# Attention with two gated MLPs behind it: a pair's value products in one run of eight, one turn later

## The chip, the cores and the metric

The kernel runs on one core of one Trainium2 chip. The metric is the device time of one execution in microseconds (us); the median of three runs of the kernel before is 1239.47 us (1239.21 to 1240.27). Five engines work beside each other, each through its own list of instructions in order: TensorE (PE, matrix products and transposes; PEld is its weight load), VectorE (DVE), ScalarE (ACT), GpSimd (POOL) and SyncE (SP, whose queue issues most of the DMAs). They meet at semaphores.

## The reference

```python
def _attn_ref(q, k, v, g_q, g_k):          # 4 batches, 12 heads, 448 positions, 64 wide
    q_n, k_n = (rmsnorm(q, g_q), rmsnorm(k, g_k))
    scores = scale * np.matmul(q_n, k_n.transpose(0, 1, 3, 2))
    scores = scores - np.max(scores, axis=-1, keepdims=True)
    attn = np.exp(scores)
    attn = attn / (np.sum(attn, axis=-1, keepdims=True) + 1e-09)
    return np.matmul(attn, v).astype(np.float32)
...
    x = np.ascontiguousarray(attn_out.transpose(0, 2, 1, 3)).reshape(B * S, H * D)
    x = _moe_ref(x=x, **moe_kwargs)        # (x @ w_a) * (x @ w_b) @ w_out
    return _moe2_ref(x=x, **moe2_kwargs)   # sigmoid(x @ w_gate) * (x @ w_val) @ w_out
```

The change lies in the attention. The two MLPs behind it take the rest of the time.

## The kernel before

The attention works on 24 pairs of heads (two heads of one batch, 64 columns each, side by side in 128 partitions). The 448 positions of a head are three chunks of 128 and a rest of 64; the rests of both heads share a chunk. For a pair, the scores are made in seven pieces of 128 x 448 (`s`, four products on PE), each with its row maximum (`top`, DVE) and its exponential (`exp`, ACT, which also adds up the rows). The exponentials must be transposed before they can be multiplied with v: `x_tr(i, j, z)` transposes chunk j in two parts z on PE, into a tile of PSUM, and `x_out` copies that to `pt` in SBUF (ACT for z = 0, DVE for z = 1). `pv(i, part)` multiplies: part 0 takes the chunks j = 0 and 1 of both heads, part 1 takes j = 2 and the shared rest j = 3. Each of these products is two PE instructions with 64 columns of weights, so a part is eight instructions and a pair sixteen. They add up in one PSUM tile `pv`. `norm` (DVE) multiplies it with the reciprocal sums `rs`, which come by way of `rsum` (DVE), `rsum_tr` (a transpose on PE), `rsum_post` (a copy on ACT at L390 and a DMA to DRAM) and `rsum_get` (DMAs that spread the row over the partitions); `put` stores the result.

The Tile framework is told to keep the order in which the functions are called (a manual schedule), so the tuples `begin`, `first`, `turns` and `end` set the order of work by hand: an entry (f, o, ...) calls f for pair i + o. `first` is turn i = 1, `turns` the turns 2 to 22, `end` the rest, in which the first MLP begins. In a turn the scores and exponentials of pair i are made, the exponentials of pair i - 1 transposed, and q and k of pair i + 2 normalised (`mean`, `rsqrt`, `newton`, `scale`) and transposed (`t_tr`), with `k_hi`, `k_lo`, `q_hi`, `q_lo` as their evictions from PSUM on ACT and DVE. From turn 6 on `decode` puts two steps of the first MLP's weight preparation into a turn (L639 on ACT; L640, L642, L646 on DVE). In the turns 15 to 20 `early_hi` (L428, ACT) and `early_lo` (L434, POOL) split finished columns of the attention for the first MLP.

Buffers that matter: all transposes (`x_tr`, `t_tr`, `rsum_tr`, ten tiles in a turn) share three PSUM tiles (`ps_tr`); the scores have four (`ps_s`), `pv` one; `pt` has four buffers for the chunks 0 to 2 and two for the rest; `v` has three.

Lines in the profile: x_tr is L339 and L342 for j < 3 (a turn's first transpose is the L339 of x_tr(-1, 0, 0)) and L344 to L347 for j = 3; x_out is L356 on DVE and L358 on ACT; s L311, top L317, exp L329, pv L371, rsum_tr L385, t_tr L264 to L269, k_hi L284, q_hi L274, norm L406, mean L213 and L214, rsqrt L221 and L222.

Of the kernel before, what the change touches and what calls it, by code (L numbers as in the profile page):

```python
# [23 lines left out]
def attention_then_two_gated_mlps(  # L24
# [90 lines left out]
    def attention():  # L115
# [336 lines left out]
        def mlp(i, n):  # L452
# [20 lines left out]
            (scale, 2, 0), (scale, 2, 2), (top, 0, 5), (rsum, -1), (exp, 0, 5), (x_tr, -1, 1, 0), (x_out, -1, 1, 0),  # L473
            (x_tr, -1, 1, 1), (x_out, -1, 1, 1), (s, 0, 2), (s, 0, 3), (squares, 3),
            (x_tr, -1, 2, 0), (top, 0, 2), (x_out, -1, 2, 0), (exp, 0, 2), (x_tr, -1, 2, 1), (rsum_tr, -1), (top, 0, 6), (exp, 0, 6),
            (x_out, -1, 2, 1), (rsum_post, -1), (pv, -1, 0), (top, 0, 3), (t_tr, 2, 1), (exp, 0, 3), (mean, 3), (rsqrt, 3), (x_tr, -1, 3, 0),
            (k_hi, 2), (newton, 3), (k_lo, 2), (t_tr, 2, 0), (x_out, -1, 3, 0), (q_hi, 2), (q_lo, 2), (k_ends, 2),
        )

        turns = (  # L480
            (rsum_get, -2), (early, 0), (put, -3), (s, 0, 0), (s, 0, 1),
            (x_tr, -1, 0, 0), (x_tr, -1, 0, 1), (top, 0, 0), (x_out, -1, 0, 0), (exp, 0, 0), (top, 0, 4),
            (exp, 0, 4), (x_out, -1, 0, 1), (pv, -2, 1), (scale, 2, 1), (scale, 2, 0), (scale, 2, 2), (top, 0, 1),
            (exp, 0, 1), (load, 4), (load_r, 3), (load_v, 1), (x_tr, -1, 1, 0), (top, 0, 5), (rsum, -1), (exp, 0, 5),
            (x_out, -1, 1, 0), (x_tr, -1, 1, 1), (norm, -2), (x_out, -1, 1, 1), (s, 0, 2),
            (s, 0, 3), (decode, 0, 0), (early_hi, -1), (squares, 3), (early_lo, -1), (x_tr, -1, 2, 0),
            (top, 0, 2), (x_out, -1, 2, 0), (exp, 0, 2), (x_tr, -1, 2, 1), (rsum_tr, -1), (top, 0, 6), (exp, 0, 6), (x_out, -1, 2, 1), (rsum_post, -1),
            (pv, -1, 0), (top, 0, 3), (t_tr, 2, 1), (exp, 0, 3), (decode, 0, 1), (mean, 3), (rsqrt, 3), (x_tr, -1, 3, 0),
            (k_hi, 2), (newton, 3), (k_lo, 2), (t_tr, 2, 0), (x_out, -1, 3, 0), (q_hi, 2), (q_lo, 2), (k_ends, 2),
        )  # L490

        end = (
            (rsum_get, -3), (put, -4), (s, -1, 0), (s, -1, 1), (x_tr, -2, 0, 0), (x_tr, -2, 0, 1), (top, -1, 0),
            (exp, -1, 0), (rsum, -2), (x_out, -2, 0, 0), (top, -1, 4), (exp, -1, 4), (x_out, -2, 0, 1), (pv, -3, 1),
            (top, -1, 1), (exp, -1, 1), (x_tr, -2, 1, 0), (top, -1, 5), (x_out, -2, 1, 0), (x_tr, -2, 1, 1),
            (exp, -1, 5), (x_out, -2, 1, 1), (rsum_tr, -2), (norm, -3), (s, -1, 2), (rsum_post, -2), (s, -1, 3),
            (x_tr, -2, 2, 0), (top, -1, 2), (x_out, -2, 2, 0), (exp, -1, 2), (x_tr, -2, 2, 1), (top, -1, 6),
# [767 lines left out]
    with tc.manual_schedule():  # L1265
        main = mlps()
        attention()
        open_places(6, 4, 2, 3)
        begin_mm("mm1", 3)
        for c in range(KC):  # L1270
            stage_in(0, "A22", c)
        ready[0] = True
        for _ in main:
            pass
# [29 lines left out]
```

## Time and profile before

| | |
|---|---|
| median of three runs | 1239.47 us (1239.21 to 1240.27) |
| the profiled execution | 1240.79 us, span 1239.0 us |
| granted TensorE clock, mean over the span | 0.990 |
| busy in the span: PE, DVE, ACT, POOL | 1199.2, 923.9, 653.5, 158.0 us |
| turns 2 to 22 of the attention | from 39.42 to 267.34 us |

The profiled execution is one run with the hardware profiler; its span reaches from the first to the last instruction, and 1.8 us lie around it. Times in the rows are microseconds from the start of the span. A group of rows in order of time shows a start, a duration, the engine, the line, the operation, the tiles it writes and reads, the shapes and how many like instructions follow each other (x6); in brackets stands the idle time of the engine ahead of it and what ended it.

### The profile page before, as it was taken

Reading aid. Unit: us, or ns where it says so; the run is one execution under the profiler, and the core shown is the slowest. Engines: PE = TensorE matmul, PEld = TensorE weight load, DVE = VectorE, ACT = ScalarE, POOL = GpSimd, SP = SyncE. Lnnn points to the kernel's source line nnn. Section 1 sums busy time; section 2 is a strip of 40 time slices with the busy share of each in tenths; the row PEclk is TensorE's granted clock in tenths of the full one; section 3 lists DMA queues with packets and bytes.
Section 4 is the critical chain, followed back from the end, with each engine's and each line's share of the span. In section 5 each row is a group of like instructions: output and inputs, shape, how many; then the busy total and the mean of one; then the engine's idle time right before and its main releaser. Section 6 shows DMA issues by size and latency. Waiting matters only on the chain.

```text
span 1239.0 us, 18146 instructions
## 1 busy us (share of the span) xinstructions
PE 1199.2 (97%) x6414; PEld 1013.5 (82%) x6414; DVE 923.9 (75%) x1621; ACT 653.5 (53%) x1271; POOL 158.0 (13%) x240
## 2 busy tenths in 40 slices
PE   4999999999899999999999999999999999999997
PEld 3666666667688888888888888788888888999997
DVE  6788889964976786876668789966876877666572
ACT  4778787873643444334445565544445344444542
POOL 4656667700000000000000000000000000000000
PEclk9999999999899999999999999999999999999999
DMA  5244455327134664653865664224654654867583
GB/s 131 74 133 127 136 152 155 119 68 266 48 100 136 189 194 142 195 174 124 305 219 188 196 216 131 94 88 135 195 190 142 207 162 137 280 215 250 170 270 101
DMA packets 142026, 203.00 MB, mean 164 GB/s; under 512 B 23240, under 2 KB 116592, under 8 KB 141936
## 3 DMA queue, kind: packets, MB, share of 16 engines
q1 hardware_dynamic: 140496, 201.26, 51.5%
q8 instruction: 50, 0.82, 0.3%
q10 hardware_dynamic: 1440, 0.59, 0.2%
q14 instruction: 40, 0.33, 0.1%
HBM read 147.46 MB, written 54.35 MB: 163 GB/s over the span
## 4 chain that ended last, share of the span: by engine, by line
PE 67%; DVE 3%; ACT 2%; DMA 1%; issue 1%; SPq 0%; ACTq 0%; DVEq 0%
PE mm L899 44%; PE mm L1176 12%; PE mm L1186 10%; DVE xl L576 1%; DMA u<-gd 0%; DMA wd<-d 0%; SPq L1242 0%; DVE u L812 0%; ACT xh L803 0%; DVE al L812 0%; DVE wl L576 0%; ACTq L1242 0%; ACT mm L1157 0%; ACT ah L1213 0%; ACT gh L1092 0%
## 5 line engine op out<-in xcount | busy, mean ns | idle before, releaser
L899 PE MATMUL mm<-xh,wh 128*128 128x512 f32 (+1 forms) x1008 | 370.2, 367 | 5.6 <-ACT u L955 2.0
L899 PE MATMUL mm<-xl,wh 128*128 128x512 f32 (+1 forms) x1008 | 370.7, 368 | 4.2 <-DVE xl L576 4.2
L899 PE MATMUL mm<-xh,wl 128*128 128x512 f32 (+1 forms) x1008 | 371.8, 369 | 1.1 <-DVE wl L576 1.1
L899 PEld LDWEIGHTS mm<-xh,wh 128*128 128x128 f32 x1008 | 190.8, 189 | 31.2 <-ACT u L955 2.3
L899 PEld LDWEIGHTS mm<-xl,wh 128*128 128x128 f32 x1008 | 190.7, 189 | 28.6 <-DVE xl L576 5.9
L899 PEld LDWEIGHTS mm<-xh,wl 128*128 128x128 f32 x1008 | 190.5, 189 | 23.4 <-DVE wl L576 2.3
L576 DVE TENSOR_TENSOR wl<-d,wh 128x384 fp32r<-128x384 f32 x252 | 137.7, 553 | 74.0 <-ACT wh L1055 45.1
L744 ACT CAST wh<-d 128x384 fp32r<-128x384 f32 x168 | 83.0, 513 | 107.3 <-DVE d L732 75.1
L646 DVE SCALAR_TENSOR_TENSOR d<-d,raw 128x384 uint32<-128x384 uint32 x140 | 82.0, 586 | 52.0 <-ACT d L639 46.1
L639 ACT ACTIVATE d<-raw 128x384 f32<-128x384 f32 x140 | 76.8, 554 | 75.3 <-DMA raw<-in_moe_w_out_dram 42.0
L329 ACT ACTIVATE P<-s,nm 128x448 f32<-128x448 f32 x168 | 105.3, 636 | 9.0 <-DVE nm L317 8.5
L1055 ACT CAST wh<-d 128x384 fp32r<-128x384 f32 x84 | 43.2, 514 | 119.6 <-issue 39.2
L1186 PE MATMUL mm<-wh,gh 128*128 128x384 f32 x294 | 99.4, 338 | 2.5 <-ACT al L1201 2.2
L317 DVE TENSOR_REDUCE nm<-s 128x1 f32<-128x448 f32 x168 | 97.5, 615 | 3.5 <-PE s L311 3.5
L1186 PE MATMUL mm<-wl,gh 128*128 128x384 f32 x294 | 99.3, 338 | 0.0
L1186 PE MATMUL mm<-wh,gl 128*128 128x384 f32 x294 | 99.2, 337 | 0.0
L1176 PE MATMUL mm<-gl,wh 128*128 128x512 f32 x252 | 92.6, 368 | 0.0
L1176 PE MATMUL mm<-gh,wl 128*128 128x512 f32 x252 | 92.4, 366 | 0.0
L1176 PE MATMUL mm<-gh,wh 128*128 128x512 f32 x252 | 91.7, 364 | 0.0
L642 DVE SCALAR_TENSOR_TENSOR raw<-raw 128x384 uint32<-128x384 uint32 x140 | 78.2, 559 | 4.0
L358 ACT COPY pt<-tr 128x512 f32<-128x512 f32 x96 | 55.0, 573 | 44.8 <-PE tr L342 40.9
L969 DVE TENSOR_TENSOR u<-mm,u 128x896 f32<-128x896 f32 x48 | 52.2, 1088 | 30.5 <-PE mm L899 30.4
(149 smaller groups left out, 1938.4 us busy)
## 6 DMA issues: line engine op xcount, KB each, us to landing
gd<-u SPq DMA_DIRECT2D x60, 448.0 KB
u<-gd SPq DMA_DIRECT2D x60, 448.0 KB
d<-wd SPq DMA_DIRECT2D x132, 192.0 KB
raw<-in_moe_w_out_dram SPq DMA_DIRECT2D x48, 384.0 KB
wd<-d SPq DMA_DIRECT2D x72, 192.0 KB
raw<-in_moe_w_a_dram SPq DMA_DIRECT2D x24, 384.0 KB
raw<-in_moe_w_b_dram SPq DMA_DIRECT2D x24, 384.0 KB
raw<-in_moe_w_val_dram SPq DMA_DIRECT2D x23, 384.0 KB
```

Source lines behind the costliest of these rows:

```text
L317: nc.vector.tensor_reduce(out=d["nm"][:, t:t + 1], in_=d["ps"][t], axis=AX.X, op=ALU.max, negate=True)
L329: nc.scalar.activation(out=e, in_=d["ps"].pop(t), func=AF.Exp, bias=d["nm"][:, t:t + 1], accum_out=d["sum"][:, t:t + 1])
L358: nc.scalar.copy(out=d["pt"][j][:, w], in_=tr)
L576: eng.tensor_tensor(out=lo, in0=t, in1=f32(hi), op=ALU.subtract)
L639: nc.scalar.activation(out=f32(t), in_=f32(high), func=AF.Copy, scale=2.0 ** -112)
L642: nc.vector.scalar_tensor_tensor(out=low, in0=high, scalar=0x80000000, in1=low, op0=ALU.bitwise_and, op1=ALU.bitwise_or)
L646: nc.vector.scalar_tensor_tensor(out=t, in0=t, scalar=3, in1=low, op0=ALU.logical_shift_left, op1=ALU.bitwise_or)
L744: nc.scalar.copy(out=hi, in_=t)
L899: nc.tensor.matmul(ps[:, o:o + size], w[:, P * c:P * c + P], x[:, o:o + size], start=(p in (1, 5) and c == 0 and z == 0), stop=(c == KC - ...
L969: nc.vector.tensor_tensor(out=u, in0=ps, in1=u, op=ALU.add)
L1176: nc.tensor.matmul(ps[:, o:o + size], w[:, P * un:P * un + P], g[:, o:o + size], start=(p in (1, 5) and f == 0 and z == 0), stop=(f == HF ...
L1186: nc.tensor.matmul(ps[:, o:o + HB], g[:, P * t:P * t + P], w, start=(p in (1, 5) and f == 0 and z == 0), stop=(f == HF - 1 and z == 2), sk ...
```

## The change

In `first` and `turns` the entry `(pv, -1, 0)`, which stood behind `rsum_post`, is gone. In `turns` `(pv, -2, 0)` stands in front of `(pv, -2, 1)` in the next turn, behind `x_out(-1, 0, 1)`; in `end` `(pv, -3, 0)` in front of `(pv, -3, 1)`. So in the turns both parts of a pair, eight products in sixteen instructions, follow each other. The last two pairs are multiplied in `end` as before.

```diff
@@ first
-            (x_out, -1, 2, 1), (rsum_post, -1), (pv, -1, 0), (top, 0, 3), (t_tr, 2, 1), (exp, 0, 3), (mean, 3), (rsqrt, 3), (x_tr, -1, 3, 0),
+            (x_out, -1, 2, 1), (rsum_post, -1), (top, 0, 3), (t_tr, 2, 1), (exp, 0, 3), (mean, 3), (rsqrt, 3), (x_tr, -1, 3, 0),
@@ turns
-            (exp, 0, 4), (x_out, -1, 0, 1), (pv, -2, 1), (scale, 2, 1), (scale, 2, 0), (scale, 2, 2), (top, 0, 1),
+            (exp, 0, 4), (x_out, -1, 0, 1), (pv, -2, 0), (pv, -2, 1), (scale, 2, 1), (scale, 2, 0), (scale, 2, 2), (top, 0, 1),
...
-            (pv, -1, 0), (top, 0, 3), (t_tr, 2, 1), (exp, 0, 3), (decode, 0, 1), (mean, 3), (rsqrt, 3), (x_tr, -1, 3, 0),
+            (top, 0, 3), (t_tr, 2, 1), (exp, 0, 3), (decode, 0, 1), (mean, 3), (rsqrt, 3), (x_tr, -1, 3, 0),
@@ end
-            (exp, -1, 0), (rsum, -2), (x_out, -2, 0, 0), (top, -1, 4), (exp, -1, 4), (x_out, -2, 0, 1), (pv, -3, 1),
+            (exp, -1, 0), (rsum, -2), (x_out, -2, 0, 0), (top, -1, 4), (exp, -1, 4), (x_out, -2, 0, 1), (pv, -3, 0), (pv, -3, 1),
```

## Rows read from the trace of the kernel before

**Rows 1.** Busy by stretch: turns 2-14, 15-21, 17, 22 (columns in the first row).

```profile
core 0: us, PE busy (x) PEld busy (x) DVE busy (x) ACT busy (x) POOL busy (x), PEclk, DMA share, GB/s
39.42:178.69 139.27, 139.27 (x951) 89.40 (x949) 119.64 (x277) 107.99 (x309) 84.86 (x132) 1.00 0.45 127
178.69:257.57 78.88, 75.50 (x513) 48.15 (x511) 70.65 (x145) 62.33 (x167) 54.64 (x73) 1.00 0.44 134
201.10:212.93 11.83, 10.82 (x74) 6.88 (x74) 10.88 (x23) 8.96 (x25) 8.71 (x11) 1.00 0.53 153
257.57:267.34 9.77, 9.77 (x67) 5.94 (x65) 6.87 (x15) 6.65 (x19) 0.00 (x0) 1.00 0.22 68
```

**Rows 2.** PE in order of time, turn 10 (start, us, engine, line).

```profile
125.13 0.33 PE L339 MATMUL tr<-ident,P 128*128 128x128 f32 x1
...
127.86 0.82 PE L342 MATMUL tr<-ident,P 128*128 128x128 f32 x6
...
130.12 0.27 PE L339 MATMUL tr<-ident,P 128*128 128x128 f32 x1
...
130.88 0.27 PE L385 MATMUL tr<-ident,rc 128*7 128x128 f32 x1
131.09 1.72 PE L371 MATMUL pv<-pt,v 128*64 128x448 f32 x8
132.74 0.55 PE L264 MATMUL tr<-ident,qkn 128*128 128x128 f32 x3
...
133.89 0.49 PE L264 MATMUL tr<-ident,qkn 128*128 128x128 f32 x3
...
135.84 0.33 PE L339 MATMUL tr<-ident,P 128*128 128x128 f32 x1
```

**Rows 3.** ACT in order of time, second half of turn 10.

```profile
130.76 0.59 ACT L358 COPY pt<-tr 128x512 f32<-128x512 f32 x1 [0.99 <-PE tr L342]
...
132.47 0.24 ACT L390 COPY row<-tr 7x128 f32<-7x128 f32 x1
132.62 0.62 ACT L329 ACTIVATE P<-s,nm 128x448 f32<-128x448 f32 x1
...
134.56 0.52 ACT L358 COPY pt<-tr 128x448 f32<-128x448 f32 x1
```

**Rows 4.** All engines in order of time, second half of turn 11.

```profile
141.80 0.56 DVE L356 COPY pt<-tr 128x384 f32<-128x384 f32 x1
...
142.80 0.55 DVE L646 SCALAR_TENSOR_TENSOR d<-d,raw 128x384 uint32<-128x384 uint32 x1
...
145.07 0.52 ACT L358 COPY pt<-tr 128x448 f32<-128x448 f32 x1
```

**Rows 5.** ACT in order of time, second half of turn 2.

```profile
45.05 0.59 ACT L358 COPY pt<-tr 128x512 f32<-128x512 f32 x1 [0.95 <-PE tr L342]
...
48.43 0.52 ACT L358 COPY pt<-tr 128x448 f32<-128x448 f32 x1
```

**Rows 6.** All engines in order of time, turn 17's end and turn 18's first transpose.

```profile
208.67 1.96 DVE L646 SCALAR_TENSOR_TENSOR d<-d,raw 128x384 uint32<-128x384 uint32 x1
...
212.35 0.52 ACT L358 COPY pt<-tr 128x448 f32<-128x448 f32 x1
...
212.93 0.33 PE L339 MATMUL tr<-ident,P 128*128 128x128 f32 x1 [1.01 <-ACT pt L358]
```

**Rows 7.** Weight loads (PEld) of turn 10's run of products, behind its first four.

```profile
131.52 0.14 PEld L371 LDWEIGHTS pv<-pt,v 128*64 128x64 f32 x2 [0.23 <-issue]
131.89 0.14 PEld L371 LDWEIGHTS pv<-pt,v 128*64 128x64 f32 x2 [0.23 <-issue]
```

**Rows 8.** DVE in order of time, turn 10, norm (L406) and x_out(2,1) (L356).

```profile
128.61 0.62 DVE L406 TENSOR_TENSOR xs<-pv,rs 128x448 f32<-128x448 f32 x1 [0.33 <-DMA rs<-dr]
...
131.15 0.54 DVE L356 COPY pt<-tr 128x384 f32<-128x384 f32 x1
```

**Rows 9.** ACT in order of time, end of turn 1.

```profile
38.46 0.52 ACT L358 COPY pt<-tr 128x448 f32<-128x448 f32 x1
```

## The prediction, made before the changed kernel was run

> **What bounds the kernel now.** The page gives TensorE (PE) by far the largest share of busy time. A share is an average over stages, so I read next the busy time of each engine in stretches of the attention [rows 1]. I call the stretch between the first transposes of two turns of the loop a turn. From 39.42 to 178.69, turns 2 to 14, PE has no idle time at all: 139.27 us busy of 139.27, 10.71 us a turn, VectorE (DVE) 119.64, ScalarE (ACT) 107.99. From 178.69 to 257.57, turns 15 to 21, PE is idle for 3.4 of 78.88 us. So for thirteen turns PE's own list is the bound; then something else joins in. Third, I read PE in order of time through turn 10 [rows 2] and ask of each step whom it waits for and who waits for it. Fourth, I follow ACT and DVE from the eviction x_out(2,0) to the eviction x_out(3,0) [rows 3 to 5]: there each step waits for the one before it. Last, the turns in which PE does wait show what closes the circle: a turn's first transposes started 0.06 us after the last turn's x_out(3,0) had ended (212.35 + 0.52 to 212.93), with 1.01 us of idle PE put down to it [rows 6]. Transposes write to three tiles in PSUM, and here the new turn takes the one that x_out(3,0) empties.
>
> The reader should see two things. In turn 10 the chain from x_out(2,0) at 130.76 ends with x_out(3,0) at 134.56 + 0.52 = 135.08, and PE comes to the next turn only at 135.84: 0.76 us of slack [rows 2, 3]. And PE spends the middle of that chain, 131.09 to 132.74, on the four value products (eight PE instructions) of pv(-1, 0). This filler is what the change takes out.
>
> **What the change does to PE's work.** No instruction is added or removed, no DMA is touched; each pair's eight instructions of part 0 go from behind rsum_tr to a place ahead of part 1 in the next turn.
> - Taken out: from rsum_tr at 130.88 to t_tr(2, 1) at 132.74 PE takes 1.86 us [rows 2]. Without the run the next transpose follows at the pitch of transposes, 0.11 (six of them took 0.82 from 127.86, the last alone 0.27: 0.55 / 5). That saves 1.75, and about 0.05 more because the first transpose after products is slow (125.13 is 0.33 long, 130.12 and others 0.27).
> - Put in: a run of eight takes 1.65 (131.09 to 132.74), of which the first pair step takes 0.43 (131.09 to 131.52) and an inner one 0.37 [rows 2, 7]. Eight more inside a run are four inner steps, 4 x 0.375 = 1.50.
> - Balance: 1.80 - 1.50 = 0.30 us less PE work a turn, 10.41 for 10.71: one entry and one exit of a run saved.
>
> The Trainium skill, "TensorEngine Tiling (Array Packing)", section Key Properties, has a rule that fits this: changing the tiling mode drains the array, and the products use 64-column tiles where the transposes use 128. The trace agrees (0.20 us from rsum_tr to the first product, 0.11 between transposes). If PE's work alone counted, that rule would make the kernel faster by the second rival's amount.
>
> **What it does to the order.** All that PE does between x_tr(1,0) and rsum_tr comes 1.50 us later in its turn. Counted from the turn's first transpose, x_tr(2,0) goes from 130.12 - 125.13 = 5.00 to 6.50 [rows 2]. ACT's x_out(2,0) follows it by 0.64 (130.12 to 130.76), so it goes to 7.14; ACT waits there for PE already now, 0.99 us [rows 3], so nothing on ACT takes the delay up. DVE's x_out(2,1) goes from 141.80 - 135.84 = 5.96 to 7.46 [rows 2, 4]. Ahead of it on DVE stand the norm, which reads the products, then x_out(1,1), a weight step and two maxima, and all of them wait for PE in turn. With the norm's own 0.62 they take 131.15 - 128.61 = 2.54 us, so about 2.0 from x_out(1,1) on [rows 8]; x_tr(1,1) ends at 128.68 - 125.13 = 3.55 now [rows 2] and at 5.06 then, so they are through at 7.1, covered by 7.46; without that cover each tenth over would go into the turn. The issue of v's load on the SP queue waits for the products, as now, 1.5 us later; behind it stand loads that are wanted a turn or more later: nothing.
>
> From there the chain is as long as it is now, and three circles close on the next first transpose:
> - Turns in which ACT decodes weights (line 639, between the exponentials and the rsqrt): 134.56 + 0.52 - 130.76 = 4.32 [rows 3]. 7.14 + 4.32 + 0.05 = **11.51**.
> - Turns in which DVE does (L646): from x_out(2,1) at 141.80 to 145.07 + 0.52 = 3.79 [rows 4]. 7.46 + 3.79 + 0.05 = **11.30**.
> - Turns without weights: 48.43 + 0.52 - 45.05 = 3.90 [rows 5], so 11.09. There PE itself is later: t_tr(2, 0) takes the PSUM tile that the copy of the sums (L390) frees, and that copy ends 132.47 + 0.24 - 130.76 = 1.95 after x_out(2,0) starts [rows 3], at 9.09; from t_tr(2, 0) to the next turn PE needs 135.84 - 133.89 = 1.95 [rows 2], and one slow first step of 0.05. 9.09 + 0.05 + 2.00 = **11.14**.
> All three exceed 10.71 although PE has less to do: with the filler gone from where the evictions run, PE has transposes alone for three buffers, and waits.
>
> **The sum**, made against the profiled run:
> - Turn 1 loses a run and gains none. Its x_out(3,0) ends at 38.46 + 0.52 = 38.98 behind a chain that the run isn't part of, so turn 2 starts at 39.04 for 39.42: -0.4 [rows 1, 9].
> - Turns 2 to 5 have no weights: 4 x (11.14 - 10.71) = +1.7.
> - Turns 6, 8, 10, 12, 14 have L639: 5 x 0.80 = +4.0. Turns 7, 9, 11, 13 have L646: 4 x 0.59 = +2.4.
> - Turns 15 to 21 last 78.88 [rows 1]. In 15 to 20 ACT and GpSimd (POOL) also prepare the next stage. In turn 17 L646 took 1.96 us, beside POOL's L434, for 0.55 in turn 11 [rows 4, 6], and the turn lasted 11.83 [rows 1]. L434 doesn't move within such a turn, so L646 starts later and ends at the same point: 11.83 in 15, 17 and 19, 11.51 in 16 and 18, 11.14 in 20 and 21. Together 80.8: +1.9.
> - Turn 22 has no t_tr and lasts 9.77, all of it PE [rows 1]. Its second half of s needs the PSUM tile of exp(0, 3), which ends 132.62 + 0.62 - 130.76 = 2.48 after x_out(2,0) starts [rows 3], and takes 0.71 itself (half of the 1.42 that is left of those 1.95 behind the four transposes): 7.14 + 2.48 + 0.05 + 0.71 = 10.38: +0.6.
> - The end, where PE has no gap either, has one run longer by 1.50: +1.5.
> Sum: -0.4 + 1.7 + 4.0 + 2.4 + 1.9 + 0.6 + 1.5 = **+11.7 us**. The MLPs behind are unchanged and PE's, so all of it reaches the end. The profiled run took 1240.79, 1.3 above the median of the runs: 1252.5 for a profiled run, **1251.2** for the median.
>
> **The rivals.**
> 1. Milder. If the new turn's first transposes take another PSUM tile than x_out(3,0)'s, the copy of the sums alone binds: 11.14 in turns 2 to 14, 13 x 0.43 = 5.6; 15 to 21 at least 1.5, turn 1 and the end as above: +8.8, 1248.3. For it: the order in which tiles come free isn't written in the kernel. Against: the waits of this kind name x_out(3,0) [rows 6].
> 2. Faster: the cover holds. If the chain behind x_out(2,0) fits into the new turn, PE stays the bound and 0.30 is saved in the 17 turns outside 15 to 19: -5.1, 1234.4. It decides where the chain takes under 10.41 - 7.14 - 0.05 = 3.2 us; the rows say 3.8 to 4.3, and on ACT its steps run end to end.
> 3. Heavier: the norm waits for the sums that a DMA spreads (rs). In turn 10 it did, 0.33 us. The sums leave ACT 1.50 us later in a turn. The cover left on DVE is 7.46 - 7.06 = 0.4; a landing 0.9 us beyond what the norm can bear costs 0.5 in each of the nine turns with weights: +4.3, 1255.5. For it: that one wait. Against: it is the only one of its size.
> That the products don't become one run can be left out: the operands of all eight are from the turn before.
>
> The Trainium skill, "Perfetto Trace Analysis", section Optimization Strategy, says that one gap repeating on the engine that should be saturated can mean too few buffers. Turns 2 to 14 show no such gap now; by my sum each gets 0.7 to 1.1 us of them.
>
> **Chances.** Forecast 0.68, milder 0.14, heavier 0.08, the cover holds 0.06, loss and saving cancel 0.04. About 0.2% (2.5 us) is what a measurement can tell from no change: faster 0.06, same 0.04, slower 0.90. The range runs from 1243.5 (milder, with the turns without weights hardly delayed and 15 to 22 as before) to 1257.0 (heavier); some 0.17 lies outside.
>
> **What would show it.** In the changed trace: 16 value products end to end in about 3.16 us; turns of 11.1 to 11.5 us from 39 us on; idle PE ahead of the first transposes put down to x_out(3,0), and ahead of t_tr; x_out(2,0) 7.1 us into a turn; turn 17 still near 11.8. Turns of 10.4 without gaps would show the second rival, turns over 11.6 with DVE waiting for rs the third. I am wrong if PE waits in fewer places, or if the start of the MLPs takes some of the delay back.

## The result, and the profile after

The changed kernel takes **1254.18 us** (median of four runs, 1252.39 to 1255.54) against 1239.87 (1239.21 to 1241.31) for the kernel before beside it: 1.0108 times as long, interval [1.0095, 1.0121]. That is +14.3 us where +11.7 was forecast (1251.2, range 1243.5 to 1257.0). The profiled execution took 1254.91 us.

The first reading is that of [rows 1]: busy time by stretch. The rows are turns 2 to 5 (no weights), 6 to 14 (weights), 15 to 21 (weights and the next stage), then turn 17 alone and turn 22.

```profile
core 0: us, PE busy (x) PEld busy (x) DVE busy (x) ACT busy (x) POOL busy (x), PEclk, DMA share, GB/s
39.29:83.89 44.60, 43.28 (x292) 27.80 (x292) 35.35 (x81) 32.80 (x93) 25.39 (x40) 1.00 0.35 99
83.89:187.57 103.68, 98.06 (x659) 62.58 (x658) 85.89 (x197) 78.17 (x217) 59.34 (x90) 1.00 0.45 128
187.57:268.50 80.93, 76.08 (x511) 48.70 (x512) 65.95 (x144) 63.60 (x168) 54.99 (x74) 1.00 0.44 130
210.95:222.81 11.86, 10.90 (x73) 6.96 (x74) 10.19 (x23) 9.13 (x25) 8.75 (x11) 1.00 0.52 154
268.50:279.14 10.64, 10.12 (x66) 6.08 (x65) 8.14 (x18) 7.26 (x21) 0.10 (x1) 1.00 0.21 64
```

TensorE had no idle time in turns 2 to 14 before; now it is idle for 1.32 us of turns 2 to 5 and for 5.62 us of turns 6 to 14. It is no longer the bound there, and neither is another engine: DVE is busy for 85.89 of 103.68. What is left is a chain across engines.

PE in order of time through turn 10, the turn of [rows 2]:

```profile
130.15 0.33 PE L339 MATMUL tr<-ident,P 128*128 128x128 f32 x1
...
131.06 2.48 PE L371 MATMUL pv<-pt,v 128*64 128x448 f32 x12
133.37 0.92 PE L371 MATMUL pv<-pt,rz 128*64 128x448 f32 x4
134.22 0.33 PE L339 MATMUL tr<-ident,P 128*128 128x128 f32 x1
...
136.67 0.27 PE L339 MATMUL tr<-ident,P 128*128 128x128 f32 x1
...
137.43 0.27 PE L385 MATMUL tr<-ident,rc 128*7 128x128 f32 x1
138.03 0.52 PE L264 MATMUL tr<-ident,qkn 128*128 128x128 f32 x3 [0.33 <-ACT pt L358]
138.90 0.33 PE L344 MATMUL tr<-swap,P 128*128 128x128 f32 x1
139.50 0.49 PE L264 MATMUL tr<-ident,qkn 128*128 128x128 f32 x3
...
141.93 0.33 PE L339 MATMUL tr<-ident,P 128*128 128x128 f32 x1 [0.42 <-ACT pt L358]
```

The sixteen products run end to end from 131.06 to 134.22, 3.16 us as worked out. Where eight of them stood before, between rsum_tr (L385) and t_tr(2, 1) (L264), PE now waits 0.33 us for x_out(2, 0), and at the end of the turn 0.42 for x_out(3, 0) (L358 both). ACT through the second half of that turn, the rows of [rows 3]:

```profile
137.30 0.59 ACT L358 COPY pt<-tr 128x512 f32<-128x512 f32 x1 [1.39 <-PE tr L342]
...
139.12 0.24 ACT L390 COPY row<-tr 7x128 f32<-7x128 f32 x1
139.41 0.64 ACT L329 ACTIVATE P<-s,nm 128x448 f32<-128x448 f32 x1
140.03 0.53 ACT L639 ACTIVATE d<-raw 128x384 f32<-128x384 f32 x1
...
141.36 0.52 ACT L358 COPY pt<-tr 128x448 f32<-128x448 f32 x1
```

x_out(2, 0) starts 137.30 - 130.15 = 7.15 us into the turn (7.14 forecast), x_out(3, 0) ends at 141.88, and the next turn's first transpose starts 0.05 later. The lengths of all turns, each from first transpose to first transpose:

| | before | forecast | after |
|---|---|---|---|
| turns 2 to 5 | 10.71 | 11.14 | 11.15, 11.16, 11.13, 11.16 |
| turns 6, 8, 10, 12, 14 (L639) | 10.71 | 11.51 | 12.13, 11.50, 11.78, 11.51, 11.50 |
| turns 7, 9, 11, 13 (L646) | 10.71 | 11.30 | 11.31 or 11.32 each |
| turns 15, 17, 19 | 11.12, 11.83, 11.85 | 11.83 | 11.88, 11.86, 11.88 |
| turns 16, 18 | 11.29, 11.30 | 11.51 | 11.50, 11.50 |
| turns 20, 21 | 10.75, 10.74 | 11.14 | 11.17, 11.14 |
| turn 22 | 9.77 | 10.38 | 10.64 |

The first product of the MLPs comes at 293.31 for 280.00: 13.3 of the 14.1 us between the two profiled executions lie in the attention.

### The profile page after: what moved, and what is told of

It reads as the page before. It is cut to its first block, busy times and chain, and to the rows that moved or that the text cites. A ratio compares the mean times of both kernels' runs of the same rounds, so it can differ in the third digit from the quotient of the medians.

```text
span 1253.1 us, 18146 instructions
## 1 busy us (share of the span) xinstructions
PE 1201.4 (96%) x6414; PEld 1014.7 (81%) x6414; DVE 921.3 (74%) x1621; ACT 657.6 (52%) x1271; POOL 158.2 (13%) x240
## 4 chain that ended last, share of the span: by engine, by line
PE 66%; DVE 3%; ACT 2%; DMA 1%; issue 1%; SPq 0%; ACTq 0%; DVEq 0%
PE mm L899 44%; PE mm L1176 12%; PE mm L1186 10%; DVE xl L576 1%; DMA wd<-d 1%; DVE u L812 0%; SPq L1242 0%; ACT xh L803 0%; DVE al L812 0%; DVE wl L576 0%; ACTq L1242 0%; DMA d<-wd 0%; ACT mm L1157 0%; ACT ah L1213 0%; ACT gh L1092 0%
## 5 line engine op out<-in xcount | busy, mean ns | idle before, releaser
L576 DVE TENSOR_TENSOR wl<-d,wh 128x384 fp32r<-128x384 f32 x252 | 138.2, 555 | 73.2 <-ACT wh L1055 41.5
L639 ACT ACTIVATE d<-raw 128x384 f32<-128x384 f32 x140 | 76.8, 554 | 77.1 <-DMA raw<-in_moe_w_out_dram 42.8
L646 DVE SCALAR_TENSOR_TENSOR d<-d,raw 128x384 uint32<-128x384 uint32 x140 | 79.5, 568 | 49.6 <-ACT d L639 43.9
L358 ACT COPY pt<-tr 128x512 f32<-128x512 f32 x96 | 54.7, 570 | 53.7 <-PE tr L342 50.0
L642 DVE SCALAR_TENSOR_TENSOR raw<-raw 128x384 uint32<-128x384 uint32 x140 | 78.1, 558 | 4.0
```

The source lines that it names most:

```text
L358: nc.scalar.copy(out=d["pt"][j][:, w], in_=tr)
L576: eng.tensor_tensor(out=lo, in0=t, in1=f32(hi), op=ALU.subtract)
L639: nc.scalar.activation(out=f32(t), in_=f32(high), func=AF.Copy, scale=2.0 ** -112)
L642: nc.vector.scalar_tensor_tensor(out=low, in0=high, scalar=0x80000000, in1=low, op0=ALU.bitwise_and, op1=ALU.bitwise_or)
L646: nc.vector.scalar_tensor_tensor(out=t, in0=t, scalar=3, in1=low, op0=ALU.logical_shift_left, op1=ALU.bitwise_or)
```

## The experiments

The theory is the forecast's: x_tr(2, 0) comes 1.50 us later in the turn, the cover of eight products is gone from the place where the evictions run, and three buffers for ten transposes let the chain from x_out(2, 0) set the turn. Against it stand: the time goes with the number of products moved (a cost of the longer run itself); one of the circles alone decides; the products' place is innocent and the filler could stand anywhere. All ratios are to the kernel before, run beside the experiment.

### Half of the change: only the chunk j = 1 moves

```diff
-            for j in (2 * part, 2 * part + 1):
+            for j in ((0,), (2, 3), (1,))[part]:
...
-            (exp, 0, 4), (x_out, -1, 0, 1), (pv, -2, 1), (scale, 2, 1), ...
+            (exp, 0, 4), (x_out, -1, 0, 1), (pv, -2, 2), (pv, -2, 1), (scale, 2, 1), ...
```

(Made on the kernel before; its `(pv, -1, 0)` stays and is now four instructions. In `end` the part 2 goes with part 1 for the pair -3 and with part 0 for the others.)

> The kernel before, with only the products of chunk j = 1 moved to the front of the next turn's run; those of j = 0 stay late: runs of twelve and four instructions in place of sixteen (or eight and eight). Theory (the late run hides the chain from x_out(2,0) to x_out(3,0), and the loss starts only when the chain's end passes PE): x_out(2,0) comes 0.75 us later, at 6.39 us of the turn; 6.39 + 4.32 + 0.05 = 10.76 in turns with L639, PE's own 10.71 in the others; so turns 2 to 14 stay at 10.71 to 10.78 and the whole gains or loses under 1.5 us: about 1240.5. Rival (each product that is made early costs its share): half of the 14 us, about 1247, turns of 11.0 to 11.1. Rival (two runs with entries and exits are as dear here): the same 10.71, it says nothing on the chain.

Measured: 1243.71 us, ratio 1.0018 [1.0006, 1.0030]. Turns 3 to 5 and 7 to 14 last 10.71 to 10.77, as the theory wants; a cost in proportion would have made them 10.9 to 11.1. So the delay is absorbed up to the slack, and it is the other half that costs. The total is 2.4 us longer all the same, and in the profiled execution (1245.53) that lies elsewhere: turn 6 lasts 11.81, turn 15 11.81 (11.12 before), the end 0.75 more, and turn 2 12.38 (the last section). Turn 6 is a case by itself: DVE waits there for the first weights (L640, the first step on them).

```profile
93.42 0.37 DVE L640 TENSOR_SCALAR raw<-raw 128x384 uint32<-128x384 uint32 x1 [1.34 <-DMA raw<-in_moe_w_a_dram]
```

The turn starts at 84.27, so this step starts 9.15 us into it; in the kernel before it was 90.31 - 82.27 = 8.04.

### The weight step moved behind the chain

Three kernels with `(decode, 0, 1)` behind `k_ends`: on the changed kernel, on the kernel before, and on the changed kernel with `rsqrt` and `newton` behind `x_out(-1, 3, 0)` and `rsum_post` ahead of `(top, 0, 6), (exp, 0, 6)` as well.

```diff
-            (top, 0, 3), (t_tr, 2, 1), (exp, 0, 3), (decode, 0, 1), (mean, 3), (rsqrt, 3), (x_tr, -1, 3, 0),
-            (k_hi, 2), (newton, 3), (k_lo, 2), (t_tr, 2, 0), (x_out, -1, 3, 0), (q_hi, 2), (q_lo, 2), (k_ends, 2),
+            (top, 0, 3), (t_tr, 2, 1), (exp, 0, 3), (mean, 3), (rsqrt, 3), (x_tr, -1, 3, 0),
+            (k_hi, 2), (newton, 3), (k_lo, 2), (t_tr, 2, 0), (x_out, -1, 3, 0), (q_hi, 2), (q_lo, 2), (k_ends, 2), (decode, 0, 1),
```

> The changed kernel, with the turn's second weight step (decode 0, 1: L639, L640, L642, L646) behind the last eviction q_lo, and so out of the chain. Theory: every turn from 2 to 21 then closes on the copy of the sums, 11.14 us: turns 6 to 14 last 100.3 us (103.7 in the changed kernel), turns 15 to 19 55.7 (58.6): 6 us less than the changed kernel, about 1248, still 8 slower than before. Rival (the loss lies in the long run itself, in norm and the maxima behind it, which wait for x_tr(1,1)): moving the weight step changes nothing much, within 1.5 us of the changed kernel, or it gets slower as the step now stands ahead of the next turn's maxima.

> The kernel before, with the same move of the turn's second weight step behind q_lo. Theory: turns 2 to 14 are PE's and stay at 10.71; in turns 15 to 19 the long DVE step beside L434 leaves the chain, PE's 3.4 us of idle time there go to nearly nothing, and these turns fall to about 10.75: 3.3 us faster than before, about 1236.5. Rival (the idle time of turns 15 to 19 comes from POOL and the ACT cast themselves): within 1 us of before.

> The changed kernel with a short chain: the second weight step behind q_lo as in the last but one, rsqrt and newton behind x_out(3,0), and the copy of the sums (rsum_post) ahead of the second exponential. Same work, same products in one run. Theory: x_out(3,0) then ends 3.5 us after x_out(2,0) starts, at 10.66, and the copy no longer binds; what is left is t_tr(2,1)'s wait for the tile of x_out(2,0) (0.4 us): 7.77 + 1.15 + 0.53 + 1.42 = 10.87 a turn in all turns. About 1241, 13 us under the changed kernel: nearly all of the loss goes although the products stay where they are. Rival (the place of the products is what costs): it stays over 1250. Rival (three PSUM tiles bind whatever the order): 11.1 a turn, 1247.

Measured: 1260.43, 1.0154 [1.0139, 1.0169]; 1256.49, 1.0125 [1.0103, 1.0147]; 1261.67, 1.0159 [1.0143, 1.0174]. All three miss. Turns 2 to 5 came out as expected (11.15 in the first, 10.93 in the third), but from turn 7 on the first has turns of 11.5 to 14.0. The kernel before shows why, since it loses 1.25% by this edit alone. SP and DVE in order of time in its turn 14, which starts at 177.08 (the weight step at its head belongs to turn 13):

```profile
178.13 0.79 DVE L646 SCALAR_TENSOR_TENSOR d<-d,raw 128x384 uint32<-128x384 uint32 x1
...
178.95 0.38 SPq L628 DMA_DIRECT2D raw<-in_moe_w_b_dram  x1
...
179.42 1.73 SPq L399 DMA_DIRECT2D rs<-dr  x3
...
185.02 0.62 DVE L406 TENSOR_TENSOR xs<-pv,rs 128x448 f32<-128x448 f32 x1 [2.22 <-DMA rs<-dr]
```

The weight step issues the load of the next raw weights. That load waits for L646 to be done with the buffer, and stands on the SP queue ahead of the DMAs that spread the sums; so the sums leave late, 179.42 - 177.08 = 2.34 us into the turn where in the kernel before they leave 1.1 us ahead of it, and the norm waits 2.22 us for them. I had moved the step and left its DMA out of the account. These kernels say little about the change itself; they do show that the third rival's mechanism (the norm waiting for rs) is there once something delays rs.

### The chain made shorter, with the weight step left inside the turn

Two parts. The row: `rsum_post` ahead of `(top, 0, 6), (exp, 0, 6)`. The chain: x_out(3, 0) ahead of decode, rsqrt and newton.

```diff
-            (top, 0, 2), (x_out, -1, 2, 0), (exp, 0, 2), (x_tr, -1, 2, 1), (rsum_tr, -1), (top, 0, 6), (exp, 0, 6), (x_out, -1, 2, 1), (rsum_post, -1),
-            (top, 0, 3), (t_tr, 2, 1), (exp, 0, 3), (decode, 0, 1), (mean, 3), (rsqrt, 3), (x_tr, -1, 3, 0),
-            (k_hi, 2), (newton, 3), (k_lo, 2), (t_tr, 2, 0), (x_out, -1, 3, 0), (q_hi, 2), (q_lo, 2), (k_ends, 2),
+            (top, 0, 2), (x_out, -1, 2, 0), (exp, 0, 2), (x_tr, -1, 2, 1), (rsum_tr, -1), (rsum_post, -1), (top, 0, 6), (exp, 0, 6), (x_out, -1, 2, 1),
+            (top, 0, 3), (t_tr, 2, 1), (exp, 0, 3), (x_tr, -1, 3, 0),
+            (k_hi, 2), (t_tr, 2, 0), (x_out, -1, 3, 0), (decode, 0, 1), (mean, 3), (k_lo, 2), (rsqrt, 3), (newton, 3), (q_hi, 2), (q_lo, 2), (k_ends, 2),
```

Both parts on the changed kernel:

> The changed kernel with the products where the change put them and the chain shortened, the weight step still inside the turn ahead of the next turn's DMAs: x_out(3,0) follows exp(0, 3) and k_hi at once; decode, mean, rsqrt and newton stand behind it; the copy of the sums stands ahead of the second exponential. Theory (the loss is the chain behind x_out(2,0), uncovered): what is left is t_tr(2,1)'s wait for the tile of x_out(2,0); 10.87 by my sum, 10.94 as turns 2 to 6 of the fourth run showed; so 10.9 to 11.0 in turns 2 to 21, about 1243.5, ten under the changed kernel. Rival (the place of the products itself costs): over 1250.

The chain alone (first line of the diff left as it was):

> As the first of this group, but with the copy of the sums left where it was. Theory: of the circles only this copy's is left: 11.14 to 11.16 in all turns from 2 to 21 (11.31, 11.5 and 11.88 go): 6 us under the changed kernel, about 1248. If the copy's circle were not there, it would fall to 10.94 as the first one.

The row alone (first line only):

> The changed kernel with the copy of the sums alone moved ahead of the second exponential. Theory: the copy binds only the turns without weights, and there the chain to x_out(3,0) stands 0.05 behind it: 11.10 for 11.14 in six turns, nothing in the others: the same as the changed kernel within 1 us, 1253 to 1254. Rival (the PSUM tile of the sums is the main wait): 1247 or less.

Both on the kernel before:

> The kernel before with the same shortened chain. Theory: turns 2 to 14 are PE's and stay at 10.71; the idle time of turns 15 to 19 goes, as the long DVE step beside L434 no longer stands ahead of x_out(3,0): 3 to 3.8 us faster than before, about 1237. Rival (as in the third run, the order of the weight steps carries a cost of its own): slower than before.

| changed kernel with | median | ratio | turns without weights | L639 | L646 |
|---|---|---|---|---|---|
| nothing more | 1254.18 | 1.0108 [1.0095, 1.0121] | 11.13 to 11.16 | 11.50 (turn 6, 12.13; turn 10, 11.78) | 11.31 |
| the row | 1253.89 | 1.0102 [1.0085, 1.0119] | 11.06 | 11.48 to 11.50 (turn 6 too) | 11.30 to 11.33 (turn 7, 12.00) |
| the chain | 1249.83 | 1.0064 [1.0049, 1.0079] | 11.14 to 11.17 | 11.14 to 11.17 | 11.14 to 11.17 |
| both | 1245.15 | 1.0020 [1.0011, 1.0029] | 10.94 | 10.94 (turn 14, 11.61) | 10.93 to 10.96 |

The columns are the turns 2 to 5, then the even and the odd ones of 6 to 14. With both parts the turns 16, 18 and 20 last 11.04 to 11.15.

This separates the circles. With the chain short, every turn lasts 11.14 to 11.17, whether it has weights or not (turn 14, 11.39, and turn 2, below, apart): the copy of the sums binds, at the 11.14 the forecast gave it. With the row short, turns without weights fall to 11.06, which is x_out(3, 0)'s circle, 11.09 in the forecast, while turns with weights stay (turn 7 apart, see the last section). The row alone gains nothing that the totals can tell (0.06%), the chain 0.4%; both gain 0.9%. The row and, below, the kernel before came out as expected in all; the chain and both have the turns that were expected, with totals 1.7 to 1.8 us longer. With both, a third wait is left. PE in order of time, turn 10 of the kernel with both:

```profile
134.03 0.27 PE L385 MATMUL tr<-ident,rc 128*7 128x128 f32 x1
134.64 0.52 PE L264 MATMUL tr<-ident,qkn 128*128 128x128 f32 x3 [0.33 <-ACT pt L358]
...
137.71 0.33 PE L339 MATMUL tr<-ident,P 128*128 128x128 f32 x1
```

From rsum_tr to t_tr(2, 1) it takes 134.64 - 134.03 = 0.61 where the pitch of transposes is 0.11 [rows 2]: 0.50 us wait for x_out(2, 0) to empty its tile. 10.94 less 0.50 is 10.44, the 10.41 of PE's work but for a slow first step.

On the kernel before the same edit gives 1237.05, 0.9962 [0.9947, 0.9977]. PE then has no idle time from turn 2 to 20, and even turns 15 to 19 last 10.71:

```profile
39.40:250.00 210.60, 210.60 (x1434) 134.85 (x1434) 187.96 (x419) 169.38 (x468) 138.95 (x202) 1.00 0.48 134
```

So the chain had something to give in the kernel before as well: the waits of turns 15 to 19, 3.8 us in all. The first product of the MLPs comes at 276.42 for 280.00. With the chain edit on both sides the change costs 0.9962 to 1.0020, 0.6%; without it 1.1%.

### Other work in the gap

If the missing cover is the cause, it need not be products that cover. The scores' piece 3, `(s, 0, 3)`, is 0.70 us of PE work and stood ahead of x_tr(2, 0). (A piece is three products on PE, one instruction each here, where the section on the kernel before says four.) On the changed kernel, one edit:

```diff
-            (s, 0, 3), (decode, 0, 0), (early_hi, -1), (squares, 3), (early_lo, -1), (x_tr, -1, 2, 0),
-            (top, 0, 2), (x_out, -1, 2, 0), (exp, 0, 2), (x_tr, -1, 2, 1), (rsum_tr, -1), (top, 0, 6), (exp, 0, 6), (x_out, -1, 2, 1), (rsum_post, -1),
+            (decode, 0, 0), (early_hi, -1), (squares, 3), (early_lo, -1), (x_tr, -1, 2, 0),
+            (top, 0, 2), (x_out, -1, 2, 0), (exp, 0, 2), (x_tr, -1, 2, 1), (rsum_tr, -1), (s, 0, 3), (top, 0, 6), (exp, 0, 6), (x_out, -1, 2, 1), (rsum_post, -1),
```

> The changed kernel with one edit: s(0, 3), three score products that take 0.71 us of PE, moves from ahead of x_tr(2,0) to behind rsum_tr, where the value products stood. The chain, the products' place and every amount of work stay. Theory (what counts is that PE reaches x_tr(2,0) early and has other work between it and the transposes that need its tiles): x_out(2,0) comes 0.71 earlier, at 6.42 of the turn; turns with L639 close at 6.42 + 4.32 + 0.05 = 10.8, those with L646 at about 10.9 (x_out(2,1) is then bound by the maxima, at 7.1), those without weights on PE at 10.4 to 10.5; turns 15 to 19 keep 11.3 to 11.9. About 1244, ten under the changed kernel. Rival (the late place must hold the value products, or the loss is the early run's): no change, 1253 to 1255; slower still if top(0, 3) and exp(0, 3), which now start later against s(0, 3), end last.

Measured: 1244.41, 1.0032 [1.0021, 1.0043], so 0.76% of the 1.08% come back by 0.70 us of work put elsewhere in the same turn. It works twice: x_tr(2, 0) comes 5.80 us into the turn (132.71 - 126.91) for 6.52 (136.67 - 130.15), and the scores cover the first eviction. Turns without weights last 10.49 to 10.52, with L639 10.84 or 10.85 (turn 6, 11.46), with L646 10.94; turns 15 to 19 last 11.33 to 11.88, as expected.

And with the short chain as well (`(s, 0, 3)` between `(rsum_tr, -1)` and `(rsum_post, -1)`):

> The fifth run's kernel (the change with the shortened chain) with the same move of s(0, 3) behind rsum_tr. Theory: with the chain shortened and the wait for x_out(2,0)'s tile covered, nothing is left but PE's list, which the change made 0.30 us shorter: 10.41 to 10.5 in turns 2 to 21 for 10.71; against the sixth run's kernel 20 x 0.25 = 5 us less, given back in part by turn 22 and the end (+0.9, +1.5): 1233 to 1235. Rival (the saving of a run's entry and exit does not reach the end): not under 1237.

Measured: **1234.61 us**, 0.9956 [0.9943, 0.9970], the fastest kernel here. PE in order of time, its turn 10, from a turn's first transpose at 122.51 to the next:

```profile
129.12 0.27 PE L385 MATMUL tr<-ident,rc 128*7 128x128 f32 x1
129.14 0.45 PE L311 MATMUL s<-KH,QH 128*128 128x448 f32 x1
...
129.84 0.49 PE L264 MATMUL tr<-ident,qkn 128*128 128x128 f32 x3
...
132.88 0.33 PE L339 MATMUL tr<-ident,P 128*128 128x128 f32 x1
```

No wait is left in it: 132.88 - 122.51 = 10.37, and so in fourteen of turns 2 to 21. The saving that the change makes in PE's work was real, 10.71 - 10.37 = 0.34 us a turn (0.30 and 10.41 forecast); it takes a chain that fits to collect it. The Trainium skill, "TensorEngine Tiling (Array Packing)", Key Properties, says that a change of tiling mode drains the array; 10.37 for 10.71 with one such change and back less in a turn agrees. Against the kernel before with the short chain (0.9962) this one is not set apart by the totals, as the intervals overlap; in the profiles the MLPs begin at 274.21 for 276.42. Turns 12, 16, 17, 18, 19 and 20 are not as short (11.50, 11.06, 10.67, 10.66, 10.43, 11.02). In turn 12 the norm waits 0.73 us, and the weight step L576 behind it takes 1.47 us, much as in turn 10 of the changed kernel (1.35, next section); the cause of the others stays open.

## Why the prediction came out as it did

**Sign, range and mechanism were right.** Point by point:

- PE's work, 3.16 us for the run of sixteen: measured 3.16. The saving of 0.30 showed as 0.34 where nothing waits (10.37).
- The delay of 1.50: x_out(2, 0) at 7.15 for 7.14.
- The circles, 11.51, 11.30 and 11.14: measured 11.50, 11.31 and 11.15 in the turns that nothing else disturbs; and the 11.09 that x_out(3, 0) would give in turns without weights, 11.06 with the row short.
- Turns 15 to 21: 80.93 us for the 80.8 forecast. Turn 17, 11.86, hardly changed, as L434's end was said to fix it.
- The end, +1.5: from the start of turn 23 to the first product of the MLPs it takes 293.31 - 279.14 = 14.17 for 280.00 - 267.34 = 12.66. Turn 1, -0.4: 16.26 for 16.64.
- "Milder" falls: x_out(3, 0) binds, as the [0.42 <-ACT pt L358] above says. "The cover holds" falls for this kernel; with the chain edit and the scores moved turns of 10.37 came about, at 1234.61 in all (this rival's 1234.4 is near by accident: turns 15 to 19 gave part of that gain, and its sum leaves out the longer run of the end, +1.5).
- "Heavier" falls as a whole: in turns 2 to 9, 11, 13 and 14 the norm starts 4.19 to 4.22 us into the turn, right behind its products, which end at 4.14. But its mechanism is there in one turn, the tenth (point 2 below), where it cost 0.3 us and not the 0.5 in each of nine turns (which make 4.5, not the 4.3 of its sum).

**The sum was 2.4 us short between the two profiled executions** (14.1 for 11.7; 2.6 by the medians). Four terms were mis-sized.

1. Turn 6, 12.13 for 11.51: +0.6. The step that failed is "behind it stand loads that are wanted a turn or more later: nothing". The SP queue issues end to end from the spread of the sums on, through the loads of q, k and v, to the first raw weights. Those are wanted in the same turn. Everything there starts with the sums, which come 1.50 us later in a turn that is 0.43 longer: 1.07. The issue of raw goes from 85.26 - 82.27 = 2.99 to 4.05 us into turn 6, and PE pays for it at the end of the turn. All engines in order of time, turn 6 of the changed kernel:

```profile
87.94 1.00 SPq L628 DMA_DIRECT2D raw<-in_moe_w_a_dram  x2
...
93.36 0.36 DVE L640 TENSOR_SCALAR raw<-raw 128x384 uint32<-128x384 uint32 x1 [0.90 <-DMA raw<-in_moe_w_a_dram]
...
94.56 0.21 ACT L221 ACTIVATE y<-ms 128x14 f32<-128x14 f32 x1 [0.49 <-DVE ms L214]
...
96.02 0.33 PE L339 MATMUL tr<-ident,P 128*128 128x128 f32 x1 [0.89 <-ACT pt L358]
```

   The wait for raw was there before (0.99 us) and cost nothing, because the chain had slack; now it delays the mean on DVE, the rsqrt on ACT by 0.49, and x_out(3, 0). The half change shows the same turn at 11.81 for 10.71, although its turns 3 to 5 and 7 to 14 are as before. In the kernel with the row alone raw is issued 3.85 us into turn 6, DVE doesn't wait for it, and the turn lasts 11.49, next to the 11.51 of the forecast. Only the first load does it: in turn 10 nothing is waited for ahead of L640.

2. Turn 10, 11.78 for 11.51: +0.3. The chain x_out(2, 0) to x_out(3, 0) takes 141.88 - 137.30 = 4.58 for the 4.32 of the forecast, as two exponentials wait for their maxima. DVE and POOL in that turn:

```profile
134.96 0.62 DVE L406 TENSOR_TENSOR xs<-pv,rs 128x448 f32<-128x448 f32 x1 [0.75 <-PE tr L342]
135.75 1.15 POOL L202 TENSOR_TENSOR sq<-sq 128x448 f32<-128x448 f32 x1
135.96 1.35 DVE L576 TENSOR_TENSOR wl<-d,wh 128x384 fp32r<-128x384 f32 x1
137.24 1.14 DVE L317 TENSOR_REDUCE nm<-s 128x1 f32<-128x448 f32 x2
```

   It begins with the norm (L406), 4.81 us into the turn for some 4.2. The row puts its wait down to transposes on PE (L342), but the norm reads none of them, and its products have ended at 134.29. The trace's semaphore records name the sums: of the sixteen parts of the last DMA that spreads them, fifteen have landed by 133.17 and the last at 134.83. That is the third rival's wait. The steps behind it move, and L576, a step on the weights, starts when GpSimd's L202, from `squares`, is under way; before, it took 0.55 here, as L202 started 0.21 us behind it. The forecast looked for such a collision with POOL only in turns 15 to 20.

3. Turn 22, 10.64 for 10.38: +0.3. The mechanism is the forecast's, as PE stops in the middle of the second half of s for exp(0, 3):

```profile
277.75 0.36 PE L311 MATMUL s<-KH,QH 64*128 64x448 f32 x1
278.34 0.47 PE L311 MATMUL s<-KH,QH 64*128 64x448 f32 x1 [0.23 <-ACT P L329]
```

   x_out(2, 0) comes 0.07 later than taken, the wait ends 0.15 after exp(0, 3) for the 0.05 put in, and from there to turn 23 it is 0.80 for 0.71.

4. The rest: the start 0.25, turns 15 to 21 0.1, and the MLPs, "unchanged and PE's, so all of it reaches the end", +0.8. Counted product by product, the shift between the two executions is 13.3 us at the first MLP product, 12.1 from some 350 us on, 13.7 after 830, 14.1 at the end. The steps lie where the granted clock differs; the one near 820 is shown in the last section. They are a difference between two executions as much as between two kernels; how much of them comes back in each run stays open.

The Trainium skill, "Perfetto Trace Analysis", Optimization Strategy, reads a gap that repeats on the engine that should be saturated as possibly too few buffers. The gaps came as said, 0.33 + 0.42 us in turn 10, and they end when an eviction empties one of three PSUM tiles. But here they went without a further buffer, by order alone: a shorter chain, and other work in the gap. A fourth tile was not tried.

## What to carry to other kernels

An engine that is 100% busy can hide a serial chain on two others that has hardly any slack (here 0.76 us in a turn of 10.71); before moving work on it, measure that chain and see what will stand beside it then. Where two circles close at nearly the same time, shortening one shows little: the two parts of the chain edit gave under 0.1% and 0.4% alone and 0.9% together. A step that is moved takes its DMA with it, and a queue that issues in order passes a delay on to loads that have nothing to do with the change.

## What was not expected of the hardware

**The granted clock falls in one execution and not in another, at the same place.** In the second MLP PE waits 2.03 us for u (L955) in both kernels, behind the same work. The changed kernel, 812 to 832 us, where PE comes back at 818.49:

```profile
812.00:822.00 10.00, 7.51 (x30) 5.80 (x29) 6.48 (x12) 6.39 (x10) 0.00 (x0) 0.88 0.31 105
822.00:832.00 10.00, 10.00 (x49) 9.08 (x48) 6.98 (x13) 4.64 (x7) 0.00 (x0) 0.95 0.20 61
```

and the kernel before, 800 to 820, where it comes back at 806.37:

```profile
800.00:810.00 10.00, 7.51 (x36) 6.13 (x35) 6.36 (x11) 6.38 (x10) 0.00 (x0) 1.00 0.31 105
810.00:820.00 10.00, 10.00 (x50) 8.82 (x49) 7.74 (x14) 5.76 (x9) 0.00 (x0) 1.00 0.28 81
```

The column PEclk is 0.88 and 0.95 in one and 1.00 in the other. PE of the changed kernel in order of time:

```profile
818.49 0.50 PE L899 MATMUL mm<-xh,wh 128*128 128x512 f32 x1 [2.03 <-ACT u L955]
...
819.29 0.39 PE L899 MATMUL mm<-xh,wh 128*128 128x512 f32 x1
...
820.27 0.63 PE L899 MATMUL mm<-xh,wh 128*128 128x512 f32 x1
```

The products keep their 0.39 us at first and then take 0.63 each: the clock went from 2.4 to 1.2 GHz for a while (PEclk is 0.50 from 820 to 823 us) when PE was already at work again. From 12.1 to 13.7, the shift grew by 1.6 us there. The same happened in turn 2 of three experiments, where PE had idled 1.82 to 2.17 us just ahead of the turn (0.72 in the changed kernel, where it did not happen): 12.38, 12.84 and 12.10 us for turns of 10.7, 11.15 and 10.5. In the kernel before, the clock fell earlier, in turn 1 (0.58 from 30 to 34 us), where the waits are long anyway. The kernel with the short chain alone, around the start of turn 2:

```profile
39.00:42.00 3.00, 2.19 (x11) 1.18 (x13) 2.71 (x8) 2.30 (x5) 2.04 (x4) 0.83 0.69 217
42.00:45.00 3.00, 3.00 (x12) 1.04 (x10) 1.83 (x6) 2.21 (x8) 2.83 (x6) 0.60 0.03 8
```

That is as large as many of the differences looked at here, so turns were compared one by one and not by the total alone.

**A DVE step of two tensors beside GpSimd: the one that starts first keeps its time.** L646 takes 0.55 us with nothing on GpSimd (turn 11 of the changed kernel). L576 took 0.55 us in turn 10 before and 1.35 after, both times with GpSimd's sum of two tensors (L202) beside it. What differs is the order of their starts. L642, a step of the same size, shows it best: the changed kernel in turn 11, where DVE is first by 0.03 us, and the kernel with the row alone in turn 7, where GpSimd is first by 0.02 us:

```profile
147.50 0.55 DVE L642 SCALAR_TENSOR_TENSOR raw<-raw 128x384 uint32<-128x384 uint32 x1
147.53 1.53 POOL L202 TENSOR_TENSOR sq<-sq 128x448 f32<-128x448 f32 x1
...
100.85 1.16 POOL L202 TENSOR_TENSOR sq<-sq 128x448 f32<-128x448 f32 x1
100.87 1.55 DVE L642 SCALAR_TENSOR_TENSOR raw<-raw 128x384 uint32<-128x384 uint32 x1
```

Where DVE is first it keeps its 0.55 us and L202 takes 1.53 for the 1.15 of other turns. Where L202 or L434 is first, these DVE steps end 0.41 or 0.42 us behind it in nine kernels (before, changed, and all experiments but the three with the weight step behind the chain, which were not read for this), in turn 10 at 137.31 for 136.90. Why they do not overlap, no run here shows. That turn 7 lasts 12.00 us for 11.31: a few hundredths of a us in the start of a DVE step can cost it 1.0.
